# A six-layer cross network on one core: VectorE's order in layer five, the third round of the last layer by pairs of blocks, and the queue of one store

## The chip, the core and the metric

The kernel runs on one core of a Trainium2 chip. The core has five engines with a queue each: TensorE (PE in the profile; PEld are its weight loads), VectorE (DVE), ScalarE (ACT), GpSimd (POOL) and SyncE (SP), which here only issues DMAs. Engines run independently and wait for each other through semaphores. Sixteen DMA engines move data between the chip's memory and the core's own; SP and ScalarE issue to them. The metric is the device time of one execution in microseconds (us), the median of several runs.

## What is computed

`x0` is 4096 rows by 416 columns, `ws` six matrices of 416 x 416, `bs` six vectors of 416, all bfloat16.

```
def reference(x0, ws, bs):
    x = x0
    for l in range(ws.shape[0]):
        x = x0 * (x @ ws[l] + bs[l]) + x
    return x
```

The kernel uses that every x is x0 times something: with c the sum of all (x @ w + b) so far, plus one, x = x0 * c. Each layer adds its product and bias to c (CM, CR in the code) and multiplies by x0 for the next layer's input (XH, XR).

## The kernel before

**Layers one to five, transposed.** In these layers features lie on the partitions and rows of the batch along the free dimension. The 416 features are three blocks m of 128 (XM0, XH, CM) and a remainder of 32 (XR, CR). The 4096 rows are two halves s of 2048, each of two tiles h of 1024. For each (s, m), TensorE fills two PSUM tiles `pt`. ScalarE adds the bias and writes `t`. VectorE adds `t` to CM (the sum) and multiplies CM by XM0 into the next layer's XH.

**Layer five (`feeding_layer`, l = 4)** feeds the last layer, whose blocks have batch rows on the partitions and features along the free dimension. So c must also be turned: for each (s, m), `rows_out` adds the last layer's bias to CM in place on VectorE (L348; for the second half of the batch only half of the columns, since there the last layer's bias comes from matmuls of `bLr` for the other blocks) and issues a DMA transpose into `XLrows` on SP's queue (L231). The remainder goes through `rem_out`, `scrR` and a copy by ScalarE (`xl_rem`). VectorE's order in this layer is written out by hand (L381 to L421) with the helpers `add` (the sum, L340), `mul` (the product, L344), `rows_out`, `rem` and `rem_out`; `pin` keeps instructions in program order. The six tiles (s, m) are called A, Bt, C (first half) and Dt, E, F (second half). The profile's VectorE rows of this layer are L340, L344, L348, L373 and L375.

**Layer six (l = LL)** works in four rounds over `quads`, pairs (s, i): each q stands for four blocks of 128 rows, one for each g. A round takes two values of q, so eight blocks u = 0 to 7. `bank[u]` is the PSUM place of block u; PAIRS, TURNS and ENDS say which half of which of four PSUM tiles that is. In PAIRS two successive blocks are neighbours in one tile; in TURNS (third round) and ENDS (fourth round) most are not. TensorE computes x @ w for each block (`mm_q_open`, `mm_q_full`, `mm_q_rem`).

For each one or two blocks, `close` calls `ew`: ScalarE casts PSUM into `t` (L505), VectorE adds XLrows (the sum, L507), and `close_product` then issues the product of the blocks before (with X0rows into `o`, L495) and its store (L496). So on VectorE the sum of one block comes before the product of the one before it. In rounds one and two blocks are closed two at a time (832 wide), in round three the first two together and then six by one (416 wide), in round four all by one. In the last round the blocks 5 to 7 get c through TensorE (`adds`), so that they need no sum, and block 7 is multiplied straight from PSUM (`direct`).

**Queues.** SP issues, in this order: transpose of A, remainder of the first half, Bt, remainder of the second half, C, Dt, E, F; then 22 stores. ScalarE's queue issues the last store, after its last cast. Buffers: six `t` (tpool), ten `o` (opool), four PSUM tiles of two banks. Completion semaphores of DMAs are eight in rotation: a store waits for the landing of the DMA that was issued eight before it.

Of the kernel before, what the change touches and what calls it, by code (L numbers as in the profile page):

```python
# [10 lines left out]
ALU = mybir.AluOpType  # L11
# [5 lines left out]
def kernel(  # L17
# [7 lines left out]
    nc = tc.nc  # L25
    B, D = x0.shape
# [19 lines left out]
    out_v = out.rearrange("(bt p) d -> p bt d", p=P)  # L46
# [11 lines left out]
    X0rows = big.tile([P, NBT, D], BF16)  # L58
# [11 lines left out]
    def col0(s, g):  # L70
        return SW * s + CW * g
# [8 lines left out]
    def pin(ins):  # L80
        tc.keep_in_program_order(ins)
# [33 lines left out]
    for g in range(1, NG):  # L115
        dst, src = WR[32 * g:32 * g + 32, 0, :], WR[0:R, 0, :]
# [113 lines left out]
    def xl_dmat(s, k):  # L230
        nc.sync.dma_start_transpose(out=XLrows[:, 16 * s:16 * s + 16, 128 * k:128 * k + 128],  # L231
                                    in_=CM[:, k, SW * s:SW * s + SW])
# [73 lines left out]
    def xl_rem(s):  # L306
        dst = XLrows[:, 16 * s:16 * s + 16, NK * P:D].rearrange("p (g i) r -> p i g r", g=NG)
        src = scrR[s][:].rearrange("p i (g r) -> p i g r", g=NG)
        n = 4 if s else 2
        for i in range(0, 4, n):  # L310
            pin(nc.scalar.copy(dst[:, i:i + n], src[:, i:i + n]))
# [13 lines left out]
    def feeding_layer(l, cur, curR, nxt, nxtR):  # L325
        tiles = [(s, m) for s in range(NS) for m in range(NK)]
        pts, ts = {}, {}

        def evict(t):
            for h in range(2):  # L330
                ts[t + (h,)] = tpool.tile([P, 2 * CW], BF16, name="t")
                nc.scalar.activation(ts[t + (h,)][:], pts[t][h][:].rearrange("p a b -> p (a b)"), ACT.Identity,  # L332
                                     bias=bM[:, t[1], l:l + 1], scale=1.0)

        def c_of(t, h):
            c0 = col0(t[0], 2 * h)
            return CM[:, t[1], c0:c0 + 2 * CW]

        def add(t, h):
            pin(nc.vector.tensor_tensor(out=c_of(t, h), in0=ts[t + (h,)][:], in1=c_of(t, h), op=ALU.add))  # L340

        def mul(t, h=0, n=2):
            c0, w = col0(t[0], 2 * h), n * CW
            pin(nc.vector.tensor_tensor(out=nxt[t[0]][:, t[1], 2 * CW * h:2 * CW * h + w], in0=CM[:, t[1], c0:c0 + w],  # L344
                                        in1=XM0[:, t[1], c0:c0 + w], op=ALU.mult))

        def last_bias(c, bias):
            pin(nc.vector.tensor_scalar(out=c, in0=c, scalar1=bias, scalar2=None, op0=ALU.add))  # L348

        def rows_out(t):  # L350
            s, m = t
            c = CM[:, m, SW * s:SW * s + SW]
            if s:
                c = c.rearrange("p (g r) -> p g r", g=NG)[:, :, 0:CW // 2]
            last_bias(c, bM[:, m, LL:L])
            xl_dmat(s, m)

        A, Bt, C, Dt, E, F = tiles
        layer_products(l, 0, tiles, pts, cur, curR, evict)
        evict(Bt)  # L360
        pr2 = psum.tile([P, 2, CW], FP32, tag="ps", name="pr2")
        for s in range(NS):
            mm_rem(l, s, pr2[:, s, :], cur, curR)
        tr = []
        for s in range(NS):
            tr.append(tpool.tile([P, 2 * CW], BF16, name="t"))
            for a in range(0, CW, CW // 2):
                nc.scalar.activation(tr[s][:, a:a + CW // 2], pr2[:, s, a:a + CW // 2], ACT.Identity, bias=bR[:, l:l + 1], scale=1.0)

        def rem(s, op):  # L370
            part = slice(CW * s, CW * s + CW)
            if op == ALU.add:
                pin(nc.vector.tensor_tensor(out=CR[:, part], in0=tr[s][:, 0:CW], in1=CR[:, part], op=op))  # L373
            else:
                pin(nc.vector.tensor_tensor(out=nxtR[:, part], in0=CR[:, part], in1=XR[0][:, part], op=op))  # L375

        def rem_out(s):
            last_bias(CR[:, CW * s:CW * s + (CW // 2 if s else CW)], bR[:, LL:L])
            nc.sync.dma_start_transpose(out=scrR[s][:], in_=CR[:, CW * s:CW * s + CW])

        add(A, 0)  # L381
        mul(A, 0)
        add(A, 1)
        add(Bt, 0)
        mul(A, 1)
        rows_out(A)
        add(Bt, 1)
        rem(0, ALU.add)
        mul(Bt, 0, 4)
        rem(0, ALU.mult)  # L390
        rem(1, ALU.add)
        rem_out(0)
        rows_out(Bt)
        rem(1, ALU.mult)

        layer_products(l, 2, tiles, pts, cur, curR, evict)
        evict(Dt)
        add(C, 0)
        add(C, 1)
        rem_out(1)  # L400
        mul(C, 0, 4)
        add(Dt, 0)
        rows_out(C)
        add(Dt, 1)
        mul(Dt, 0, 4)

        def before_last(t):
            xl_rem(0)
            evict(t)

        layer_products(l, 4, tiles, pts, cur, curR, before_last)
        evict(F)
        add(E, 0)
        rows_out(Dt)
        add(E, 1)
        mul(E, 0, 4)
        add(F, 0)
        rows_out(E)
        add(F, 1)
        mul(F, 0, 4)  # L420
        rows_out(F)  # L421
        xl_rem(1)

    cur, curR = XH[0:2], XR[1]
    for l in range(1, LL):
        nxt, nxtR = [[h for h in XH if h is not cur[0] and h is not cur[1]][0], cur[0]], XR[1 + (l % 2)]
        if l == LL - 1:
            feeding_layer(l, cur, curR, nxt, nxtR)
            cur, curR = nxt, nxtR
            break  # L430
        tiles = [(s, m) for s in range(NS) for m in range(NK)]
        pts = {}

        def finish(t):
            for h in range(2):
                ew_main(l, t[0], t[1], h, pts[t][h], nxt)

        for n in range(0, len(tiles), 2):
            layer_products(l, n, tiles, pts, cur, curR, finish)
            finish(tiles[n + 1])  # L440
            if n == 0:
                rem_pair(l, cur, curR, nxtR)
        cur, curR = nxt, nxtR

    l = LL
# [37 lines left out]
    pending = []  # L483

    def rows(q, g0, n):
        s, i = quads[q]
        b0 = 16 * s + 4 * g0 + i
        return slice(b0, b0 + 4 * (n - 1) + 1, 4)

    def close_product():  # L490
        while pending:
            src, q, g0, n, eng = pending.pop()
            b = rows(q, g0, n)
            o = opool.tile([P, 2, D], BF16, name="o")
            pin(nc.vector.tensor_tensor(out=o[:, 0:n, :], in0=src, in1=X0rows[:, b, :], op=ALU.mult))  # L495
            eng.dma_start(out_v[:, b, :], o[:, 0:n, :])  # L496

    def ew(q, g0, n, src, eng, added, direct):
        if direct:
            close_product()  # L500
            pending.append((src, q, g0, n, eng))
            return
        t = tpool.tile([P, 2 * CW], BF16, name="t")
        tv = t[:, 0:n * D].rearrange("p (a d) -> p a d", a=n)
        nc.scalar.copy(tv, src)  # L505
        if not added:
            pin(nc.vector.tensor_tensor(out=tv, in0=tv, in1=XLrows[:, rows(q, g0, n), :], op=ALU.add))  # L507
        close_product()
        pending.append((tv, q, g0, n, eng))

    PAIRS = [(0, 0), (0, 1), (1, 0), (1, 1), (2, 0), (2, 1), (3, 0), (3, 1)]
    TURNS = [(0, 0), (0, 1), (1, 0), (2, 0), (3, 0), (1, 1), (2, 1), (3, 1)]
    ENDS = [(0, 0), (1, 0), (2, 0), (0, 1), (3, 0), (1, 1), (2, 1), (3, 1)]
    rounds = [(0, PAIRS, 2), (2, PAIRS, 2), (4, TURNS, 2), (6, ENDS, 1)]
    for q, at, done in rounds:
        tiles = [psum.tile([P, 2, CW], FP32, tag="ps", name=f"py{n}") for n in range(4)]
        bank = [tiles[n][:, a, :] for n, a in at]

        final = q + 2 == NQ

        def close(u, n):
            tl, a = at[u]
            ew(q + u // 4, u % 4, n, tiles[tl][:, a:a + n, 0:D], nc.scalar if final and u == 7 else nc.sync,
               final and u >= 5, final and u == 7)

        for u in range(done):
            if q == 0:
                mm_q_open(q, u, bank[u])
            else:
                mm_q_full(q, u, bank[u], False)  # L530
        mm_q_rem(q, bank[0:4], done)
        close(0, done)
        mm_q_rem(q + 1, bank[4:8], 0)
        for u in range(done, 8):
            mm_q_full(q + u // 4, u % 4, bank[u], True, final and u >= 5)
            if at is not PAIRS:
                close(u, 1)
            elif u % 2:
                close(u - 1, 2)
    close_product()  # L540


# [28 lines left out]
```

## Time and profile before

| what | value |
|---|---|
| median of 3 runs | 129.75 us (129.72 to 129.80) |
| the profiled execution | 129.89 us, span 128.1 us |
| granted TensorE clock, mean | 0.997 |
| PE busy | 122.5 us (96%) |
| DVE busy | 102.9 us (80%) |
| ACT busy | 87.7 us (68%) |
| L495, 832 wide, x9 / 416 wide, x13 | 587 ns / 377 ns each |
| L507, 832 wide, x9 / 416 wide, x11 | 587 ns / 375 ns each |
| L505 cast, 832 wide, x9 / 416 wide, x13 | 855 ns / 506 ns each |
| stores on SP's queue | 9 of 208 KB, 13 of 104 KB |

The span is the time from the first to the last instruction of the profiled execution. Busy time counts instructions that run, not waits. PE's busy share says little by itself: matmuls overlap, and their ends are modelled. Instructions on VectorE and ScalarE overlap their neighbours a little, so the time that one adds to a full engine is its start-to-start distance, not its duration. In the timelines, a line gives the start, the length, the engine, the code line, the operation, output and inputs, and how many instructions were merged ("x2"); in square brackets is idle time before it and what ended it.

### The profile page before, as it was taken

How to read it: one execution, taken by the hardware profiler on the slowest of the kernel's cores; microseconds unless marked ns; L12 is line 12 of the kernel's file. 1: busy time of each engine (PE TensorE's matmuls, PEld its weight loads, DVE VectorE, ACT ScalarE, POOL GpSimd, SP SyncE). 2: the span in 40 equal slices, each digit the busy share in tenths (PEclk: the TensorE clock that was granted, in tenths of full speed). 3: DMA queues.
4: the chain of work that ended last, by engine and by line, in shares of the span. 5: the costliest groups of instructions: out<-in, count | busy, mean ns of one | idle time of the engine just before them, and what ended most of it. 6: DMA issues, size and time to landing. Idle time of an engine off the chain costs nothing.

```text
span 128.1 us, 3968 instructions
## 1 busy us (share of the span) xinstructions
PE 122.5 (96%) x1684; PEld 55.3 (43%) x1686; DVE 102.9 (80%) x198; ACT 87.7 (68%) x109; POOL 5.6 (4%) x18
## 2 busy tenths in 40 slices
PE   7999999999999999999999999999999999999960
PEld 3343343444445444444444445444444345445530
DVE  0124579774979898989898989898999999999990
ACT  0038867887858667858667858667859697679740
POOL 4004002500000000000000000000000000000000
PEclk9999999999999999999999999999999999999998
DMA  3999999999950000000000000000089999999764
GB/s 99 232 229 223 178 235 263 304 331 335 339 155 0 5 0 0 8 0 5 0 5 0 5 0 5 0 0 5 0 164 91 176 168 213 157 303 292 248 199 142
DMA packets 42230, 16.38 MB, mean 128 GB/s; under 512 B 31034, under 2 KB 42212, under 8 KB 42212
## 3 DMA queue, kind: packets, MB, share of 16 engines
q1 hardware_dynamic: 37432, 15.40, 53.2%
q10 hardware_dynamic: 4780, 0.72, 3.6%
q8 instruction: 13, 0.21, 0.7%
q14 instruction: 5, 0.04, 0.1%
HBM read 6.15 MB, written 3.41 MB: 75 GB/s over the span
## 4 chain that ended last, share of the span: by engine, by line
PE 86%; DMA 4%; DVE 3%; ACTq 2%; issue 1%; ACT 0%; DVEq 0%
PE pt L208 50%; PE ph L240 11%; PE py L463 10%; PE pt L214 5%; PE pr L224 5%; DMA xrig<-in_x_dram 4%; DVE t L507 2%; PE pr L220 2%; PE ph L247 1%; PE py L476 1%; DVE o L495 1%; PE py L457 1%; ACTq L86 1%; ACTq L108 1%; ACT t L505 0%
## 5 line engine op out<-in xcount | busy, mean ns | idle before, releaser
L208 PE MATMUL pt<-XH,WM 128*32 128x512 bf16 x1152 | 65.2, 379 | 0.0
L187 ACT ACTIVATE t<-pt,bM 128x1024 bf16<-128x1024 f32 x36 | 37.2, 1115 | 13.7 <-PE pt L214 13.7
L208 PEld LDWEIGHTS <-WM 128*32 128x32 bf16 x1152 | 29.7, 97 | 33.8 <-issue 5.1
L188 DVE TENSOR_TENSOR CM<-t,CM 128x1024 bf16<-128x1024 bf16 x36 | 24.7, 687 | 4.3 <-ACT t L187 4.3
L189 DVE TENSOR_TENSOR XH<-CM,XM 128x1024 bf16<-128x1024 bf16 x36 | 24.9, 692 | 2.6
L505 ACT CAST t<-py 128x416 bf16<-128x416 f32 (+1 forms) x22 | 14.2, 649 | 4.2 <-PE py L463 1.8
L463 PE MATMUL py<-WM,XH 128*128 128x416 bf16 x90 | 17.0, 339 | 0.0
L240 PE MATMUL ph<-XM,WM 128*128 128x512 bf16 x70 | 16.3, 379 | 0.3 <-DMA XM<-in_x_dram 0.2
L332 ACT ACTIVATE t<-pt,bM 128x1024 bf16<-128x1024 f32 x12 | 12.4, 1115 | 4.1 <-PE pt L214 4.1
L181 ACT ACTIVATE CM<-ph,bM 128x1024 bf16<-128x1024 f32 x12 | 12.5, 1114 | 3.5 <-PE ph L247 3.5
L183 DVE TENSOR_TENSOR XH<-CM,XM 128x512 bf16<-128x512 bf16 x24 | 8.9, 434 | 4.0 <-ACT CM L181 3.9
L463 PEld LDWEIGHTS <-XH 128*128 128x128 bf16 x90 | 8.5, 98 | 7.5 <-issue 1.2
L240 PEld LDWEIGHTS <-WM 128*128 128x128 bf16 x72 | 6.8, 98 | 8.7 <-issue 1.3
L495 DVE TENSOR_TENSOR o<-t,X0rows 128x416 bf16<-128x416 bf16 (+1 forms) x22 | 9.9, 463 | 0.0
L507 DVE TENSOR_TENSOR t<-t,XLrows 128x416 bf16<-128x416 bf16 (+1 forms) x20 | 9.3, 470 | 0.1
L340 DVE TENSOR_TENSOR CM<-t,CM 128x1024 bf16<-128x1024 bf16 x12 | 8.1, 687 | 0.3 <-ACT t L332 0.3
L344 DVE TENSOR_TENSOR XH<-CM,XM 128x2048 bf16<-128x2048 bf16 (+1 forms) x7 | 7.5, 1070 | 0.4
L214 PE MATMUL pt<-XR,WR 32*128 32x512 bf16 x96 | 7.3, 379 | 0.0
L224 PE MATMUL pr<-XH,WM 128*32 128x512 bf16 x96 | 6.6, 379 | 0.0
L196 ACT ACTIVATE t<-pr,bR 128x256 bf16<-128x256 f32 x12 | 4.7, 475 | 1.6 <-PE pr L224 1.6
L114 ACT ACT_TABLE_LOAD x1 | 1.3, 1283 | 6.1 <-DMA XM<-in_x_dram 6.1
L224 PEld LDWEIGHTS <-WM 128*32 128x32 bf16 x120 | 3.2, 97 | 3.2
(61 smaller groups left out, 59.2 us busy)
## 6 DMA issues: line engine op xcount, KB each, us to landing
X0rows<-in_x_dram SPq DMA_DIRECT2D x8, 312.0 KB, 6.7
out_dram<-o SPq DMA_DIRECT2D x9, 208.0 KB, 3.0
WM<-in_ws_dram SPq DMA_DIRECT2D x5, 312.0 KB
out_dram<-o SPq DMA_DIRECT2D x13, 104.0 KB, 1.9
X0rows<-in_x_dram SPq DMA_DIRECT2D x4, 208.0 KB, 6.3
WR<-in_ws_dram SPq DMA_DIRECT2D x4, 130.0 KB, 5.4
WM<-in_ws_dram ACTq DMA_DIRECT2D x1, 312.0 KB
XM<-in_x_dram SPq DMA_TRANSPOSE x8, 5.7
```

The source lines that it names most:

```text
L181: nc.scalar.activation(c, src, ACT.Identity, bias=bias, scale=1.0)
L187: nc.scalar.activation(t[:], src, ACT.Identity, bias=bias, scale=1.0)
L188: nc.vector.tensor_tensor(out=c, in0=t[:], in1=c, op=ALU.add)
L189: nc.vector.tensor_tensor(out=x, in0=c, in1=XM0[:, m, c0:c0 + 2 * CW], op=ALU.mult)
L208: nc.tensor.matmul(pts[g // 2][32 * q:32 * q + 32, g % 2, :], lhsT=WM[:, l, k, 128 * m + 32 * q:128 * m + 32 * q + 32], rhs=cur[s][:, k, C ...
L214: nc.tensor.matmul(pts[g // 2][:, g % 2, :], lhsT=WR[32 * g:32 * g + 32, l, 128 * m:128 * m + 128], rhs=curR[32 * g:32 * g + 32, CW * s:CW ...
L224: nc.tensor.matmul(pr[32 * g:32 * g + 32, :], lhsT=WM[:, l, k, NK * P:D], rhs=cur[s][:, k, CW * g:CW * g + CW], start=False, stop=(k == NK ...
L240: nc.tensor.matmul(pt[:, gl, :], lhsT=WM[:, 0, k, 128 * m:128 * m + 128], rhs=cur[:, k, c0:c0 + CW], start=(k == 0 and not after_row), sto ...
L332: nc.scalar.activation(ts[t + (h,)][:], pts[t][h][:].rearrange("p a b -> p (a b)"), ACT.Identity, bias=bM[:, t[1], l:l + 1], scale=1.0)
L463: nc.tensor.matmul(py[:, 0:D], lhsT=q_x(q, g, k), rhs=WM[:, l, k, :], start=((not closes) and k == 0), stop=(closes and not adds and k == ...
L505: nc.scalar.copy(tv, src)
L507: pin(nc.vector.tensor_tensor(out=tv, in0=tv, in1=XLrows[:, rows(q, g0, n), :], op=ALU.add))
```

## The change

- In layer five, the second half's sum of a tile now comes before the `rows_out` that stood in front of it (for A with Bt, C with Dt, E with F). `rows_out(F)` leaves the layer: `feeding_layer` returns it, and it is called in round one of the last layer, behind the first `close`, so behind the first sum L507 (L511 in the changed file).
- `ew` takes a list of PSUM sources. For round three (TURNS) two blocks are closed together: two casts of 416 into one `t`, one sum and one product of 832, and two stores of one block each. Rounds one, two and four are as before.
- In the last round the store of block 6 goes to ScalarE's queue, as that of block 7 did.

```diff
         add(A, 1)
         add(Bt, 0)
         mul(A, 1)
+        add(Bt, 1)
         rows_out(A)
-        add(Bt, 1)
         rem(0, ALU.add)
...
         add(Dt, 0)
+        add(Dt, 1)
         rows_out(C)
-        add(Dt, 1)
         mul(Dt, 0, 4)
...
         add(F, 0)
+        add(F, 1)
         rows_out(E)
-        add(F, 1)
         mul(F, 0, 4)
-        rows_out(F)
         xl_rem(1)
+        return lambda: rows_out(F)
...
         while pending:
-            src, q, g0, n, eng = pending.pop()
-            b = rows(q, g0, n)
+            src, q, g0, n, parts, eng = pending.pop()
             o = opool.tile([P, 2, D], BF16, name="o")
-            pin(nc.vector.tensor_tensor(out=o[:, 0:n, :], in0=src, in1=X0rows[:, b, :], op=ALU.mult))
-            eng.dma_start(out_v[:, b, :], o[:, 0:n, :])
-
-    def ew(q, g0, n, src, eng, added, direct):
+            pin(nc.vector.tensor_tensor(out=o[:, 0:n, :], in0=src, in1=X0rows[:, rows(q, g0, n), :], op=ALU.mult))
+            for j in range(0, n, parts):
+                eng.dma_start(out_v[:, rows(q, g0 + j, parts), :], o[:, j:j + parts, :])
+
+    def ew(q, g0, srcs, eng, added, direct):
         if direct:
             close_product()
-            pending.append((src, q, g0, n, eng))
+            pending.append((srcs[0], q, g0, 1, 1, eng))
             return
         t = tpool.tile([P, 2 * CW], BF16, name="t")
+        n = 0
+        for src in srcs:
+            w = src.shape[1]
+            nc.scalar.copy(t[:, n * D:n * D + w * D].rearrange("p (a d) -> p a d", a=w), src)
+            n += w
         tv = t[:, 0:n * D].rearrange("p (a d) -> p a d", a=n)
-        nc.scalar.copy(tv, src)
         if not added:
             pin(nc.vector.tensor_tensor(out=tv, in0=tv, in1=XLrows[:, rows(q, g0, n), :], op=ALU.add))
         close_product()
-        pending.append((tv, q, g0, n, eng))
+        pending.append((tv, q, g0, n, n // len(srcs), eng))
...
-        def close(u, n):
-            tl, a = at[u]
-            ew(q + u // 4, u % 4, n, tiles[tl][:, a:a + n, 0:D], nc.scalar if final and u == 7 else nc.sync,
-               final and u >= 5, final and u == 7)
+        def close(groups):
+            u, direct = groups[0][0], final and groups[0][0] == 7
+            srcs = [tiles[at[g[0]][0]][:, at[g[0]][1]:at[g[0]][1] + len(g), 0:D] for g in groups]
+            ew(q + u // 4, u % 4, srcs, nc.scalar if final and u >= 6 else nc.sync,
+               final and u >= 5, direct)
...
-        close(0, done)
+        close([range(done)])
+        if q == 0:
+            last_rows_out()
...
-            if at is not PAIRS:
-                close(u, 1)
+            if at is ENDS:
+                close([[u]])
             elif u % 2:
-                close(u - 1, 2)
+                close([[u - 1, u]] if at is PAIRS else [[u - 1], [u]])
```

More of the change, by code (lines that the diff above doesn't have):

```diff
@@ L427 @@
         if l == LL - 1:
-            feeding_layer(l, cur, curR, nxt, nxtR)
+            last_rows_out = feeding_layer(l, cur, curR, nxt, nxtR)
             cur, curR = nxt, nxtR
```

## The prediction, made before the changed kernel had run

> **What bounds the kernel now.** I read the page first, then the chain of waits, then the timelines of VectorE, ScalarE and SP's queue over the last 35 us. The page's slices (3.2 us each; PE, DVE and DMA rows) say where to look:
>
> ```profile
> PE   7999999999999999999999999999999999999960
> DVE  0124579774979898989898989898999999999990
> DMA  3999999999950000000000000000089999999764
> ```
>
> TensorE is full until the last two slices. VectorE is full over the last eleven, and the DMA engines are full for ten of these. The chain gives the end:
>
> ```profile
> 114.69 3.80 PE py L463 x21
> ...
> 119.08 0.52 ACT t L505
> ...
> 119.63 0.38 DVE t L507
> ...
> 124.28 0.79 DVE o L495 x2
> ```
>
> Up to about 119 us it runs through TensorE, then through one cast and then only through VectorE's sums (L507) and products (L495). VectorE's timeline shows how close together these stand, and what layer five costs just before (start, duration):
>
> ```profile
> 99.47 0.75 DVE L348 TENSOR_SCALAR CM<-CM,bM 128x2048 bf16<-128x2048 bf16 x1
> 100.14 0.68 DVE L340 TENSOR_TENSOR CM<-t,CM 128x1024 bf16<-128x1024 bf16 x1
> 100.92 1.23 DVE L344 TENSOR_TENSOR XH<-CM,XM 128x2048 bf16<-128x2048 bf16 x1
> ...
> 106.78 1.23 DVE L344 TENSOR_TENSOR XH<-CM,XM 128x2048 bf16<-128x2048 bf16 x1
> 108.05 0.49 DVE L348 TENSOR_SCALAR CM<-CM,bM 128x1024 bf16<-128x1024 bf16 x1
> 108.59 1.09 DVE L507 TENSOR_TENSOR t<-t,XLrows 128x832 bf16<-128x832 bf16 x2
> 109.60 0.59 DVE L495 TENSOR_TENSOR o<-t,X0rows 128x832 bf16<-128x832 bf16 x1
> ...
> 117.13 0.37 DVE L507 TENSOR_TENSOR t<-t,XLrows 128x416 bf16<-128x416 bf16 x1
> 117.42 0.59 DVE L495 TENSOR_TENSOR o<-t,X0rows 128x832 bf16<-128x832 bf16 x1
> 117.92 0.37 DVE L507 TENSOR_TENSOR t<-t,XLrows 128x416 bf16<-128x416 bf16 x1
> ...
> 124.48 0.59 DVE L495 TENSOR_TENSOR o<-py,X0rows 128x416 bf16<-128x416 f32 x1
> ```
>
> Independent neighbours overlap by 0.08 us: a 0.59 us pair costs 0.50, a 0.37 us single 0.285, a 0.69 us sum 0.60. A neighbour that works on what the one before it has just touched does not overlap: L344 at 100.92 starts 0.78 after its own sum, not 0.60. VectorE lags behind ScalarE, whose casts set how far it can catch up:
>
> ```profile
> 114.54 4.05 ACT L505 CAST t<-py 128x832 bf16<-128x832 f32 x7 [0.49 <-PE py L476]
> 119.08 0.51 ACT L505 CAST t<-py 128x416 bf16<-128x416 f32 x1 [0.48 <-PE py L480]
> 119.98 2.09 ACT L505 CAST t<-py 128x416 bf16<-128x416 f32 x4 [0.39 <-PE py L463]
> 122.27 0.51 ACT L505 CAST t<-py 128x416 bf16<-128x416 f32 x1 [0.20 <-PE py L469]
> 122.99 0.51 ACT L505 CAST t<-py 128x416 bf16<-128x416 f32 x1 [0.21 <-PE py L469]
> ```
>
> The last cast ends at 123.50 and TensorE's last product about 123.67 (L469 starts at 123.49 and takes 0.18), but the VectorE product that needs the latter starts only at 124.48. So the tail is VectorE's by 0.8 us, and that 0.8 is all that less VectorE work can bring. SP's queue is one line of transposes and stores:
>
> ```profile
> 101.06 11.13 SPq L231 DMA_TRANSPOSE XLrows<-CM  x4
> 112.29 13.23 SPq L496 DMA_DIRECT2D out_dram<-o  x22
> ```
>
> It issues its last store, the last but one of the kernel, from 125.12 to 125.52, beside ScalarE's only one (125.10 to 125.50).
>
> **The change, part by part.** Times are of the profiled execution: 129.89 us in all, its span 128.1 (128.07 to the last record), 1.8 around it; the median shown, 129.75, is 0.14 below.
>
> *Layer five.* The same instructions stand in another order. The gaps that vanish are those between dependent neighbours: L348 of A behind L344 of A (91.66, where 91.55 would do: 0.11); L344 of D behind its sum (0.18); the same for F (106.78 for 106.60: 0.18); L348 of F behind L344 of F (108.05 for 107.92: 0.13); the first L507 behind that (0.54 after its start, where such an L348 takes 0.40, from 102.67 to 103.06: 0.14). Together 0.74. Against it, the second sum of C waits for its cast: it starts at 96.93 now and the cast ends at 96.86, so 0.07 is lost. Net 0.67: the second sum of round one comes at 108.42 instead of 109.10. The bounds are 0 (nothing is added, and the transposes below are covered) and 0.74; I take 0.67, since each gap is read off the line itself. The inputs of layer six (L344) are ready earlier too, which brings nothing: no group of TensorE's matmuls there idles.
>
> What is moved past it: the transposes. A's L348 ends 0.5 us later; SP then issues nothing from 94.23 to 95.49, waiting for the remainder's bias, so that is covered, and without that idle time 0.5 would pass on to all later transposes. C's bias (a sum of 0.60 later, 0.04 gained by then) would end at 100.78, just before SP's queue is free at about 100.9. E's (0.60 later, 0.22 gained) ends at 106.46 instead of 106.08, and SP waits for it: 0.38 late, and F's transpose and the first store with it (112.67 for 112.29). F's bias now stands behind the first sum, which needs the transposes of A, B and C; C's must land by 107.5, when the sum would start (L344 of F at 106.38, plus 1.14). The transposes issued at 92.44 and 97.31 landed after 5.8 and 4.4 us, so one issued at 100.95 lands by 106.8: covered by 0.7, and each us more would be a us of VectorE. F's bias ends at 108.4, before SP has issued E's transpose (109.2): no cost. The first sum that needs F's transpose comes at 115.45; issued at 109.3 with 5.8 us it lands at 115.1.
>
> *Third round in pairs.* Of the round's seven sums and seven products one each is a pair already. Between 117.13 and 120.77 stand eleven singles and one pair: 11 x 0.285 + 0.50 = 3.64. Instead six pairs, 6 x 0.50 = 3.01, and the last product costs 0.50 for 0.285: 0.63 - 0.22 = 0.41 saved. ScalarE's casts stay as they are, and so do the stores, one block each. A pair's sum waits for two casts. The seven casts from 114.54 end at 115.40, 115.86, 116.39, 116.92, 117.44, 117.97 and 118.60 (pitch 0.53); with the lead of 0.67 the pairs' sums would come at 116.46, 117.48 and 118.63, the last two on the heels of their casts. Bounds 0.41 and, with no lead to spend, the same.
>
> *Last round.* With both gains (1.08) VectorE would run ahead of the casts: sums at 119.63, 120.52, 121.09, 121.66 and 122.23, products of units 3 to 5 at 122.52, 122.80 and 123.09. The product of unit 6 waits for its cast (123.50) until 123.53; unit 7's follows at 123.82, 0.15 behind TensorE, and ends at 124.41 instead of 125.07. So 0.66 of 1.08 reaches the end; 0.41 alone would give 124.67.
>
> *Last but one store on ScalarE's queue.* It is issued at about 123.95 for 0.40, behind all casts, so that only the last store (ready at 124.44) stands behind it: no delay. SP's queue ends one issue (0.49 pitch) earlier, at about 124.5. No row shows two stores in a row on ScalarE's queue. The nearest: stores issued on SP at 123.74 and 124.17 landed after 1.7 us, and the last two, issued at the same moment, kept the DMA engines busy until 127.0 (their share is 0.00 from there on), which makes about 2.0. Bounds 0 and 0.3; I take 0.15, the middle, since the stores no longer start together but still share the DMA engines. The Trainium skill says in "DMA: Bandwidth & Descriptors", section "Issuing engines are not separate DMA queues", that several issuing engines save only the sequencer's time to initiate; by it this part brings 0 and the sum is 0.15 less.
>
> *Sum:* 0.66 + 0.15 = 0.81 off 129.89, 129.08 in a profile; off the median 129.75, **128.95 us**.
>
> **The rivals.**
> *The order in layer five brings nothing.* For it: a gap might only turn up elsewhere. Against: independent neighbours overlap in every row shown. Then 0.41 stays, 124.67 for VectorE's end: 129.75 - 0.41 = **129.34**. The Trainium skill has such a rule in "VectorE: DVE Perf Modes", section "The DRAIN you can't avoid": the next operation waits for the empty pipe whether or not a semaphore lies between. The rows at 100.14 and 100.92 disagree with that, 0.60 against 0.78.
>
> *The DMA engines bound the end.* Their share is 1.06 from 112 to 118 us. The store of 113.98 landed after 4.3 us, that of 118.03 after 3.5, of 119.75 after 2.7, of 122.65 after 1.9: a backlog that drains only as single stores come more slowly than they are served. The stores now start 0.38 later and come earlier at the end. The ninth store landed at 118.03 + 3.5 = 121.5 and the third after it at 119.75 + 2.7 = 122.45, 0.32 each. From 121.5 + 0.38, fourteen singles at 0.32 end at 126.4, level with the forecast's 127.1 - 0.8 = 126.3. With each at 0.36 (one eighth more) it is 126.9, and 0.2 is left of the gain: **129.55**, no change.
>
> *Slower: the backlog holds the queues.* Every store waits for the landing of the one eight before, and the last but one store now stands ahead of the last on ScalarE's queue. The one eight before it is the fifth after the ninth: 121.88 + 5 x 0.32 = 123.5, 0.45 before it is needed. Once that landing slips by more than 0.45 both wait, us for us, and past 1.25 us of slip the end lies behind today's. For it: the landing time jumped from 2.5 to 4.3 us between the stores of 113.43 and 113.98; one more such jump of 1.8 there costs 1.35: 128.95 + 1.35 = **130.3**. Against: nothing in the change adds bytes, and that jump came where the engines were full.
>
> **How the numbers follow.** Forecast 0.62, no gain from the order 0.17, DMA-bound 0.13, slower 0.05; 0.03 is left for a larger gain (the full 0.8 of the tail and the 0.3). The forecast's own bounds, 0.66 + 0 to 0.66 + 0.3 and up to 0.1 of the slack behind TensorE, give 128.7 to 129.1. The range 128.65 to 129.6 takes in the first two rivals and leaves about 0.1 out. A measurement of this kernel tells 0.2%, 0.26 us, from no change, so faster means below 129.49: forecast, first rival, the larger gain and a third of the second, 0.86; same 0.08; slower 0.06.
>
> **What would show it.** L344 of D and F 0.60 to 0.67 after their predecessor; the second sum near 108.4; six 832-wide instructions between the ninth product's neighbours; no VectorE gap over 0.1 in the third round; the last product at 123.8; two issues on ScalarE's queue near 123.95 and 124.45; the first store near 112.7. It is wrong if VectorE idles before the first sum (C's transpose), if the last product still starts past 124.2, or if it starts at 123.8 and the span still ends past 127.7.

## The result, and the profile after

| | before | after |
|---|---|---|
| median of 22 runs each | 129.79 us (129.64 to 130.32) | 129.50 us (129.30 to 129.77) |
| ratio, 95% interval | | 0.9977 (0.9971 to 0.9983) |
| profiled execution | 129.89, span 128.1 | 129.49, span 127.7 |
| VectorE's last product | 124.48 to 125.07 | 123.83 to 124.42 |
| SP's last store issued / ScalarE's last | 125.12 / 125.10 | 124.34 / 124.45 |
| last landing | 127.21 | 126.69 |

The changed kernel is faster by 0.22 to 0.38 us, where 0.8 was forecast. VectorE did what was forecast; less than half of the gain forecast for the end arrived there. The page's slices of the changed kernel (3.2 us each, tenths busy):

```profile
PE   7899999999999999999999999999999999999970
DVE  0123579874979898989898989898999999999990
DMA  3999999999950000000000000000098899899864
```

VectorE is as full over the last eleven slices as before. The DMA engines' row has changed: five nines near the end where there were seven, and an 8 for a 7 from 118 to 121 us. VectorE's timeline (start, duration) shows the edits one by one:

```profile
98.84 1.28 DVE L340 TENSOR_TENSOR CM<-t,CM 128x1024 bf16<-128x1024 bf16 x2
100.05 0.74 DVE L348 TENSOR_SCALAR CM<-CM,bM 128x2048 bf16<-128x2048 bf16 x1
100.71 1.22 DVE L344 TENSOR_TENSOR XH<-CM,XM 128x2048 bf16<-128x2048 bf16 x1
...
107.51 0.58 DVE L511 TENSOR_TENSOR t<-t,XLrows 128x832 bf16<-128x832 bf16 x1
108.01 0.48 DVE L348 TENSOR_SCALAR CM<-CM,bM 128x1024 bf16<-128x1024 bf16 x1
108.41 0.58 DVE L511 TENSOR_TENSOR t<-t,XLrows 128x832 bf16<-128x832 bf16 x1
...
117.49 0.59 DVE L511 TENSOR_TENSOR t<-t,XLrows 128x832 bf16<-128x832 bf16 x1
118.54 0.59 DVE L511 TENSOR_TENSOR t<-t,XLrows 128x832 bf16<-128x832 bf16 x1
...
123.83 0.58 DVE L494 TENSOR_TENSOR o<-py,X0rows 128x416 bf16<-128x416 f32 x1
```

L344 of D (100.71) now starts 0.66 after its predecessor instead of 0.78. The second sum comes at 108.41 (108.42 was forecast), the third round's sums are pairs right behind their casts, and the last product starts at 123.83, 0.65 earlier than before. ScalarE's timeline has its last cast and the two stores:

```profile
123.00 0.51 ACT L507 CAST t<-py 128x416 bf16<-128x416 f32 x1 [0.17 <-PE py L469]
123.95 0.86 ACTq L496 DMA_DIRECT2D out_dram<-o  x2
```

The chain of waits no longer ends in a run of VectorE's sums and products. It goes through TensorE, the last cast and a single product, and from there into the closing waits:

```profile
119.32 2.39 PE py L463 x13
...
123.00 0.52 ACT t L507
...
123.54 0.07 DVE o L494
```

So VectorE is out of the way, yet the end moved by 0.40 (127.67 for 128.07 in the records). The windows of one us each (window, length, busy PE, PEld, DVE, ACT, POOL, granted clock, DMA share, GB/s) show what the DMA engines do then, first before:

```profile
122.00:123.00 1.00, 1.00 (x12) 0.69 (x11) 1.00 (x5) 0.58 (x3) 0.00 (x0) 1.00 0.48 147
...
125.00:126.00 1.00, 0.00 (x0) 0.00 (x0) 0.07 (x1) 0.00 (x0) 0.00 (x0) 1.00 0.67 216
126.00:127.00 1.00, 0.00 (x0) 0.00 (x0) 0.00 (x0) 0.00 (x0) 0.00 (x0) 1.00 0.70 221
```

and after:

```profile
122.00:123.00 1.00, 1.00 (x12) 0.67 (x11) 1.00 (x5) 0.63 (x2) 0.00 (x0) 1.00 0.52 171
...
125.00:126.00 1.00, 0.00 (x0) 0.00 (x0) 0.00 (x0) 0.00 (x0) 0.00 (x0) 1.00 1.00 306
126.00:127.00 1.00, 0.00 (x0) 0.00 (x0) 0.00 (x0) 0.00 (x0) 0.00 (x0) 1.00 0.17 57
```

Before, the stores trickle at 0.7 until the end. After, they bunch: a whole us at share 1.00, after four stores left within 0.61 us, two on SP's queue (123.84, 124.34) and two on ScalarE's (123.95, 124.45). Both have a us at half share before that (122 to 123). SP's queue shows where the hole comes from (the same timeline, cut at three windows; SPq is an issue on SP's queue):

```profile
111.76 0.94 SPq L496 DMA_DIRECT2D out_dram<-o  x1
120.59 0.88 SPq L496 DMA_DIRECT2D out_dram<-o  x2
121.01 1.29 SPq L496 DMA_DIRECT2D out_dram<-o  x2
```

Two successive issues take 0.88 together at 120.59, but 1.29 at 121.01: the queue stands still for 0.44 between 121.53 and 121.97, although the product that this store carries was done at 121.19. In the trace of before the same stop lies between its 14th and 15th store (121.22 to 121.67). The line of 22 merged stores that the prediction quoted hides it.

### The profile page after: what moved, and what is told of

Read it like the earlier page. It is cut to its first block, busy times and chain, and to the rows that moved or that the text cites. A ratio compares the mean times of both kernels' runs of the same rounds, so it can differ in the third digit from the quotient of the medians.

```text
span 127.7 us, 3953 instructions
## 1 busy us (share of the span) xinstructions
PE 122.4 (96%) x1684; PEld 55.3 (43%) x1686; DVE 102.6 (80%) x192; ACT 87.8 (69%) x109; POOL 5.0 (4%) x18
## 4 chain that ended last, share of the span: by engine, by line
PE 90%; DMA 4%; ACTq 2%; DVEq 1%; ACT 0%; issue 0%; DVE 0%
PE pt L208 50%; PE py L463 12%; PE ph L240 11%; PE pt L214 5%; PE pr L224 5%; DMA xrig<-in_x_dram 4%; PE pr L220 2%; PE py L476 2%; PE ph L247 1%; PE py L457 1%; ACTq L86 1%; DVEq L573 1%; ACTq L108 1%; ACT t L507 0%; ACTq L74 0%
## 5 line engine op out<-in xcount | busy, mean ns | idle before, releaser
L507 ACT CAST t<-py 128x416 bf16<-128x416 f32 (+1 forms) x22 | 14.2, 649 | 4.2 <-PE py L463 2.0
L494 DVE TENSOR_TENSOR o<-t,X0rows 128x832 bf16<-128x832 bf16 (+1 forms) x19 | 9.4, 503 | 0.1
L511 DVE TENSOR_TENSOR t<-t,XLrows 128x832 bf16<-128x832 bf16 (+1 forms) x17 | 8.9, 522 | 0.0
L344 DVE TENSOR_TENSOR XH<-CM,XM 128x2048 bf16<-128x2048 bf16 (+1 forms) x7 | 7.5, 1066 | 0.2
```

The lines of the kernel that those rows point to most:

```text
L507: nc.scalar.copy(t[:, n * D:n * D + w * D].rearrange("p (a d) -> p a d", a=w), src)
```

## The experiments

Each ratio is to runs of the kernel before beside it on the same chip; in brackets is its 95% interval. The theories that the expectations name: V, VectorE's gain reaches the end whole; L, the landings of the last stores, a third of a us each, set the end; Q, formed on the way, SP's queue sets it, at 0.48 us for each store issued back to back plus one stop of 0.44.

### Each part alone

**Order of layer five alone** (the kernel before with these moves):

```diff
+        add(Bt, 1)
         rows_out(A)
-        add(Bt, 1)
...
+        add(Dt, 1)
         rows_out(C)
-        add(Dt, 1)
...
+        add(F, 1)
         rows_out(E)
-        add(F, 1)
...
-        rows_out(F)
+        return lambda: rows_out(F)
...
         close(0, done)
+        if q == 0:
+            last_rows_out()
```

> The kernel before with the new order of layer five alone (F's bias behind the first sum as well); third round by single blocks, last but one store on SP. Both theories: VectorE's last product starts near 123.8 and ends near 124.4 instead of 125.07, since the lead of 0.67 alone carries it to the last cast. Theory L (the landings of the last stores set the end, at about a third of a us each, and pass on only a part of VectorE's gain): 0.2 to 0.4 us faster than before. Theory V (VectorE's gain reaches the end whole, and in the changed kernel the store on ScalarE's queue takes some of it back): 0.55 to 0.7 faster.

129.27 us, ratio 0.9958 (0.9945 to 0.9970): more than the whole change brought. By the medians (0.60 faster) this is in theory V's range and above L's. VectorE's timeline and ScalarE's store:

```profile
123.78 0.58 DVE L495 TENSOR_TENSOR o<-py,X0rows 128x416 bf16<-128x416 f32 x1
...
124.39 0.41 ACTq L496 DMA_DIRECT2D out_dram<-o  x1
```

The last product stands where the whole change has it (123.83). The last store of SP leaves at 124.55 and the last landing is at 126.50.

**Third round in pairs alone** (with `close` and `ew` as in the change):

```diff
-            if at is not PAIRS:
-                close(u, 1)
+            if at is ENDS:
+                close([[u]])
             elif u % 2:
-                close(u - 1, 2)
+                close([[u - 1, u]] if at is PAIRS else [[u - 1], [u]])
```

> The kernel before with the third round in pairs alone. Both: VectorE ends near 124.67, 0.40 earlier than before. Theory L: 0.1 to 0.25 us faster. Theory V: 0.35 to 0.45 faster.

129.96 us, ratio 1.0012 (1.0004 to 1.0020): slightly slower, where both theories expected a gain, and although VectorE ends 0.55 earlier. VectorE's last product and SP's single stores:

```profile
123.93 0.58 DVE L494 TENSOR_TENSOR o<-py,X0rows 128x416 bf16<-128x416 f32 x1
...
119.11 6.70 SPq L496 DMA_DIRECT2D out_dram<-o  x13
```

The kernel before issues the same thirteen from 118.60 on, in 6.92:

```profile
118.60 6.92 SPq L496 DMA_DIRECT2D out_dram<-o  x13
```

A pair's product gives out its first store only when both blocks are done, so the queue starts 0.51 later. After that it waits for VectorE only once, for 0.12: 13 x 0.48 + 0.44 = 6.68, measured as 6.70. SP's last issue starts at 125.42 instead of 125.12. (In these two executions the last landings are level, 127.20 and 127.21; that the pairs cost time alone rests on the medians.) In the kernel before, VectorE ended at 125.07 and SP's last store left at 125.12: two chains that ended together, and this part moves the second the wrong way. That is theory Q.

**The store of block 6 on ScalarE's queue alone** (this part of one line):

```diff
-nc.scalar if final and u == 7 else nc.sync,
+nc.scalar if final and u >= 6 else nc.sync,
```

> The kernel before with the last but one store on ScalarE's queue alone. Both: VectorE's end stays at 125.07. Theory L: the last three stores still land one after the other; between 0.1 slower and 0.1 faster. Theory V: the last store, now second on ScalarE's queue, lands 0.2 to 0.3 later after its issue: 0.1 to 0.3 slower.

130.27 us, ratio 1.0031 (1.0019 to 1.0042), slower than either theory expected. ScalarE's timeline:

```profile
124.69 1.14 ACTq L496 DMA_DIRECT2D out_dram<-o  x2
```

Two issues take 1.14 here and 0.86 in the changed kernel: ScalarE stands still for 0.33 right before the last store, which leaves at 125.47 instead of 125.10.

### One part taken out of the change

**The change with block 6's store back on SP** (`u >= 6` becomes `u >= 7`):

> The changed kernel with the last but one store back on SP's queue. Both: VectorE ends at 124.41 as in the changed kernel. Theory L: SP's queue, which issues one store in 0.48 us, ends 0.5 later than in the changed kernel, so 0.0 to 0.2 us slower than it (0.1 to 0.3 faster than before). Theory V: 0.2 to 0.3 faster than the changed kernel (0.5 to 0.6 faster than before).

129.57 us, ratio 0.9974 (0.9962 to 0.9987), against 0.9977 for the change: no gain of the store's queue is seen here, as theory L expected and not V. With these intervals a gain of 0.1 us could not be told from none. Against the order alone (0.9958) the pairs cost about 0.2 us, but the intervals overlap.

**The change without pairs** (`if at is ENDS:` becomes `if at is not PAIRS:`):

> The changed kernel with round three by single blocks (order of layer five and the store on ScalarE's queue, no pairs). Theory Q: SP's twelve singles from 118.21 end near 124.5, 0.5 before those of the kernel with the order alone; the last store on ScalarE's queue is held by 0.3 us, as in the kernel with the store alone, where ScalarE stopped just before it: 129.2 to 129.5. Theory L: as the kernel with the order alone, 129.2 to 129.35.

129.63 us, ratio 0.9986 (0.9975 to 0.9997), above what either expected. SP's last store leaves at 124.15, yet ScalarE's timeline shows its stop again before the last store:

```profile
123.95 1.12 ACTq L496 DMA_DIRECT2D out_dram<-o  x2
```

That store leaves at 124.72 and lands 2.28 later, at 127.00. With two stores on ScalarE and round three by single blocks the stop falls there; in the changed kernel, where ScalarE's trace records three instructions fewer, it falls into the closing steps instead.

### Issues on SP's queue, fewer and more

**The change with one store of 208 KB for each pair of round three:**

```diff
-        pending.append((tv, q, g0, n, n // len(srcs), eng))
+        pending.append((tv, q, g0, n, n, eng))
```

> The changed kernel with one store of 208 KB for each pair of round three instead of two of 104 KB: three issues fewer on SP, the same bytes. Theory Q (SP's queue sets the end: from the first single store on it issues one in 0.47 to 0.48 us back to back, with one stop of 0.44 us at a fixed place in its instructions): SP is no longer back to back in round three, its last store is issued by 124.1 instead of 124.34, and the last landing comes 0.2 to 0.5 us earlier: 129.0 to 129.3. Theory L (the DMA engines' own rate sets the landings at the end): same bytes at the same rate, 129.4 to 129.6.

129.28 us, ratio 0.9960 (0.9948 to 0.9972). Same work on VectorE, same bytes, three issues less: SP's last store leaves at 124.16 and the last landing is at 126.50. By the median Q's size is met; the profiled execution is the slowest of the five, 129.49.

**The same with block 6's store on SP** (`u >= 7`):

> One store for each pair of round three, and the last but one store on SP. Theory Q: SP's last store is issued near 124.5 (one issue after the 124.1 of e5), level with ScalarE's 124.45, without ScalarE's stop in its closing steps: 129.0 to 129.3, as e5. Theory L: 129.4 to 129.6.

129.46 us, ratio 0.9973 (0.9962 to 0.9983), a miss for Q and in L's range, though the interval overlaps that of the one above. The last landing is at 126.50 in both, and in both more time than before's 0.86 lies behind it, 1.05 here and 1.17 above. SP closes with five waits in a fixed order, each for two semaphores. In before the last to land is in the fourth; here it is in the first and above in the second, and the waits behind it, 0.065 each, still come. Above, ScalarE's stop adds 0.18 in the closing steps. What makes the medians differ by 0.18 is open.

**Order alone, singles on VectorE, round three's six single stores as three of two blocks** (two products go into the halves of one `o`, one store behind the second):

> The kernel with the order of layer five alone (e1), sums and products of round three by single blocks, but its six single stores issued as three of two blocks. VectorE's last product is held by the last cast as in e1. Theory Q: SP has three issues fewer; its last store is issued near 124.5 as in e8 and e1, so 129.2 to 129.5: as e8, which has the same stores with VectorE's work in pairs, within 0.15. If pairs on VectorE were themselves worth something at the end, e8 would be faster than this by 0.2 or more.

129.46 us, ratio 0.9967 (0.9956 to 0.9979), as expected and equal to the one above within the intervals. With equal stores, pairs or singles on VectorE make no difference that can be told.

**One issue more:** the change with block 6's store on SP and a transfer of 4 bytes, unused, behind one store of the last round:

```diff
+            if (q, g0) == (6, 2):
+                nc.sync.dma_start(spare[0:1, :], o[0:1, 0, 0:2])
```

> The changed kernel with the last but one store back on SP (e4) and one more DMA issue on SP in the last round, of 4 bytes, between two stores. Theory Q: everything behind it on SP is issued 0.45 later, and the end with it: 0.35 to 0.5 us slower than e4, 129.9 to 130.1. Theory L: 4 bytes cost nothing, 129.5 to 129.65.

129.88 us, ratio 1.0010 (0.9999 to 1.0021): 0.0036 or 0.47 us above the same kernel without it (129.57; by medians 0.31), far from L's range and just below Q's. SP's queue:

```profile
122.37 0.51 SPq L497 DMA_DIRECT2D out_dram<-o  x1
122.93 0.72 SPq L499 DMA_DIRECT2D spare<-o  x1
123.75 1.79 SPq L497 DMA_DIRECT2D out_dram<-o  x4
```

This issue holds the queue for 0.82 us (122.93 to 123.75), longer than a store's 0.48, and the end comes 0.3 to 0.5 us later, though 4 bytes ask nothing of VectorE and almost nothing of the DMA engines. The extra transfer also shifts the stores by one semaphore: the last to land is now in the third closing wait instead of the fourth, which explains 0.05 of it. This is the clearest support for Q.

**The first four stores of the last round as two as well,** with block 6's store on SP, then on ScalarE:

```diff
+            if q == NQ - 2:
...
+                j = g0 % 2
+                pin(nc.vector.tensor_tensor(out=o[:, j:j + 1, :], in0=src, in1=X0rows[:, rows(q, g0, n), :], op=ALU.mult))
+                if j:
+                    eng.dma_start(out_v[:, rows(q, g0 - 1, 2), :], o[:])
+                continue
```

> e8 (one store for each pair of round three, last but one store on SP) with the first four stores of the last round issued as two of two blocks as well: SP has two issues fewer in the last 2 us, its last store is issued near 123.95 to 124.1, straight after its product. Theory Q: the last landing is then that of ScalarE's store, 0.2 to 0.3 earlier than in e8: 129.1 to 129.3. If the DMA engines' rate holds the landings (theory L): as e8, 129.4 to 129.55.

> As e10, with the last but one store on ScalarE's queue. SP is done by 123.6. Theory Q: no gain over e10, since SP no longer is what is late, and ScalarE's stop of 0.35 at a fixed place in its instructions falls into the closing steps as in the changed kernel: 129.2 to 129.45, 0.0 to 0.2 slower than e10. Theory L: as e5, 129.3.

129.76 us (0.9991, 0.9981 to 1.0001) and 129.94 us (1.0003, 0.9990 to 1.0017): both missed, on the slow side. The stop now falls right before block 4's store (123.27 to 123.71 in the first), and the data of the bigger stores comes out later, so that much is still on its way at the end (argued from the traces, not tried); both land last at 126.9. Fewer issues alone are not the cure, and Q alone does not give these times.

### The stop, moved

In before, in the changed kernel and in all experiments the stop precedes the same place on SP, the 80th instruction that the trace records there, whichever store that is. Loading X0rows in more pieces, early and far from the end, puts more instructions ahead of it:

```diff
-    for q in range(12):
-        b0, b1 = NBT * q // 12, NBT * (q + 1) // 12
+    for q in range(28):
+        b0, b1 = NBT * q // 28, NBT * (q + 1) // 28
```

**20 pieces,** on the order alone, on the change, and on the change with block 6's store on SP:

> The kernel with the order of layer five alone (e1), and X0rows loaded in 20 pieces instead of 12, early in the kernel where SP has time. SP then has 16 instructions more ahead of its stores; the stop of 0.44 us, if it belongs to the 80th of SP's recorded instructions, moves eight stores forward, to a store for whose product SP waits anyway. Theory Q: SP's last store is issued at about 124.1 instead of 124.55, and the end comes 0.2 to 0.35 earlier than in e1: 128.9 to 129.1. If the stop belongs to the store and not to the place, or SP is not what is late: as e1, 129.2 to 129.35.

> The changed kernel with X0rows loaded in 20 pieces. Theory Q: SP's last store is issued near 123.9 instead of 124.34, ahead of both of ScalarE's; the last landing is ScalarE's, at 124.45 + 1.8 to 2.0 instead of 2.24: 0.2 to 0.4 earlier than in the changed kernel, 129.1 to 129.3 (ScalarE's own stop stays in the closing steps). If SP's stop does not count: 129.4 to 129.55.

> Order and pairs, last but one store on SP (e4), with X0rows loaded in 20 pieces. Theory Q: SP's last store is issued near 124.4 instead of 124.86, level with ScalarE's: 0.25 to 0.4 earlier than e4, 129.1 to 129.35. If the stop does not count: as e4, 129.5 to 129.6.

129.36 (0.9962, 0.9948 to 0.9977), 129.49 (0.9973, 0.9962 to 0.9984) and 129.44 us (0.9970, 0.9958 to 0.9983): each equal to its kernel with 12 pieces, and each above what Q expected. The stop moved by four stores only, to the 11th, still among stores issued close together: the eight more pieces are eight more recorded instructions on SP, not the sixteen expected. These runs also show that more pieces by themselves bring nothing.

**28 pieces,** on the same three:

> As e12 (order of layer five alone), with X0rows in 28 pieces. In e12 the 80th instruction was the 11th store, still among the stores that SP issues back to back; eight instructions more put it on the 7th, where SP waits for a product. Theory Q: SP's last store near 124.1 to 124.2 instead of 124.55, and the end 0.2 to 0.35 earlier than e1: 128.9 to 129.1. If SP's queue is not what holds the last landing: 129.2 to 129.4.

> The changed kernel with X0rows in 28 pieces. Theory Q: SP's last store near 123.9 instead of 124.34, last landing ScalarE's store: 129.1 to 129.3. Otherwise 129.4 to 129.55.

> Order and pairs, last but one store on SP (e4), with X0rows in 28 pieces. Theory Q: SP's last store near 124.4 instead of 124.86: 129.1 to 129.35. Otherwise 129.45 to 129.6.

The stop is now before the 7th store. It still delays that one (in the change with 28 pieces the product is done at 115.66 and the stop ends at 116.04), but early enough: SP waits 0.36 for a product again before the store of 118.75. The order alone: 129.15 us, ratio 0.9952 (0.9940 to 0.9965), 0.9958 without, between Q's range and the other. The change: 129.23 us, 0.9951 (0.9938 to 0.9964), 0.9977 (0.9971 to 0.9983) without. The change with block 6's store on SP: 129.20 us, 0.9962 (0.9949 to 0.9976), 0.9974 without. These two are in Q's ranges. Only for the change do the intervals part: 0.0026, some 0.33 us (0.15 to 0.5). SP's queue of that kernel, first the moved stop and then its twelve last stores:

```profile
115.02 1.47 SPq L496 DMA_DIRECT2D out_dram<-o  x2
118.75 5.80 SPq L496 DMA_DIRECT2D out_dram<-o  x12
```

The changed kernel's own twelve take 0.32 more:

```profile
118.61 6.12 SPq L496 DMA_DIRECT2D out_dram<-o  x12
```

Its windows have lost the hole, and less is left over for the last us:

```profile
122.00:123.00 1.00, 1.00 (x13) 0.69 (x12) 1.00 (x5) 0.77 (x2) 0.00 (x0) 1.00 0.70 229
...
125.00:126.00 1.00, 0.00 (x0) 0.00 (x0) 0.00 (x0) 0.00 (x0) 0.00 (x0) 1.00 0.95 307
126.00:127.00 1.00, 0.00 (x0) 0.00 (x0) 0.00 (x0) 0.00 (x0) 0.00 (x0) 0.71 0.05 16
```

From 122 to 123 it moves 229 GB/s where the changed kernel moves 171: 0.06 MB, half a store, that need not be moved at the end. The last landing comes at 126.55 instead of 126.69, although VectorE's last product ends 0.14 later in this execution (124.56): ScalarE's last store lands 1.96 after its issue (124.59) instead of 2.24.

No run tried what the stop is, but the traces give a hint. They also hold the packets of the DMA queues that the page calls "instruction". In every kernel the next load of 8 KB on queue q14 starts 0.6 to 1.5 us after the end of SP's stop, and it moves with the stop:

| kernel | SP's stop | next load on q14 |
|---|---|---|
| before | 121.22 to 121.67 | 122.57 |
| changed | 121.53 to 121.97 | 122.60 |
| changed, 20 pieces | 119.03 to 119.47 | 120.12 |
| changed, 28 pieces | 115.59 to 116.04 | 117.49 |

Behind ScalarE's stop there is such a load too (124.40 to 124.72 and 125.76 in the change without pairs). So the stops seem to belong to the loading of an engine's own instructions; that is a reading of the times, not shown.

## Why the prediction was half right

**Layer five: right.** The lead of 0.67 was read off the gaps, and 0.69 came (108.41 for 109.10). The order alone is worth 0.0042 or 0.55 us (0.39 to 0.71 by the interval), so the rival by which it brings nothing is out. It had the Trainium skill's "VectorE: DVE Perf Modes", section "The DRAIN you can't avoid", beside it. That section also says "A next op that is not held starts earlier", which the prediction left out; the rows of 0.66 after the move and 0.78 before it, and this run, agree with that. The covers held as well: C's transpose was in time for the first sum, and E's, issued at 106.49 (106.46 forecast), delayed no sum. The first store left at 111.76, not at 112.7, because the issue of F's transpose took 1.99 instead of 3.27.

**Third round in pairs: saving right, worth wrong.** VectorE was freed as worked out. But with the lead of layer five already there, the last casts hold VectorE (the prediction's own 0.66 of 1.08), so that the pairs could bring nothing at the end. Their price was not seen: the stores of a pair come out together and later, and SP's queue has little slack to take that up. Alone they cost 0.16 us (0.05 to 0.26).

**VectorE's end: right.** 124.41 was forecast and 124.42 came, with ScalarE's issues at 123.95 and 124.45 to the hundredth.

**The step that failed** is the one behind VectorE's end: that its 0.66 "reaches the end", with 0.15 more from the store. The last issue did come 0.67 earlier (124.45 for 125.12). But from there to its landing the last store took 2.24 instead of 2.09, so 0.15 was lost where 0.15 was to be gained, and from landing to end it took 0.98 instead of 0.86, 0.12 that the sum put at nothing. In the profiles 0.67 - 0.15 - 0.12 = 0.40 arrived of 0.81. Behind the landing term stands "SP's queue ends one issue (0.49 pitch) earlier, at about 124.5". It took SP's queue for a line that follows VectorE, and did not count the stop of 0.44 that the trace of before already has. In the changed kernel twelve stores at about 0.48 and that stop made SP end at 124.73, so that its last two stores met ScalarE's two. With the stop moved the landing took 1.96. The prediction also read the DMA row as full for ten slices; it shows an 8, seven nines and then 7, 6 and 4.

**The 0.15 for the store's queue: not seen** (0.9977 against 0.9974, with intervals that would hide it), and 0.40 us lost by itself. That fits the Trainium skill's "DMA: Bandwidth & Descriptors", section "Issuing engines are not separate DMA queues", which the prediction set beside it. The SP time saved was real (its last issue 0.5 earlier, 124.34 for 124.86), but the transfers met at share 1.00.

**How much is settled.** The stop accounts for about 0.33 us (0.15 to 0.5): that is shown by moving it, in one kernel, with 20 pieces as the control; in the other two the gains of 0.08 and 0.16 are not resolved. With 28 pieces the change stands at 0.64 us below before; the last 0.17 to the forecast is only argued from traces: three stores served a third of a us apart, landings of 2.0 to 2.3 us, and ScalarE's stop of 0.32 to 0.36, which now falls in the closing steps. SP's longest wait for another queue there is 0.56 in all five kernels where ScalarE's stop falls there, and 0.38 in all others, also in the two where it falls before ScalarE's last store. That stop was not moved by itself. The DMA-bound rival gave 129.55, next to the 129.50 measured, but part of that is luck: it put the last landing at 126.9, which came at 126.69, and left out the closing. Its mechanism is part of the cause: 4 bytes more on the queue cost 0.3 to 0.5 us, so the engines alone don't set the end, but with the stop out of the way they still run at share 0.95 from 125 to 126, so their rate is a bound there too.

The rival on the slower side, a jump in the landings that holds the queues, did not occur. The versions that beat both kernels are the change with 28 pieces, 129.23 us, and the order of layer five with 28 pieces, 129.15 us. The second does without pairs and without the store on ScalarE.

## What to carry to other kernels

When one engine ends last by a few tenths of a us, look for the next chain that ends as late, and count a queue's issues one by one, not by a merged line: here a line of 22 merged stores hid a stop of 0.44 us and a queue that ended within 0.1 us of VectorE. Work done in pairs saves time on its engine but hands on its results later and together, which is a loss if a queue behind it is full. A part that is worth 0.55 us alone can be worth half with two others beside it, so the parts should be run alone.

## What the runs showed of the hardware that was not expected

- SP's queue stands still for 0.43 to 0.45 us before the 80th instruction that its trace records, in all 19 kernels, whatever that instruction is. ScalarE does so for 0.32 to 0.36 us before its 192nd recorded one in the seven kernels with two stores on its queue; in five more the 192nd comes where ScalarE waits for another queue anyhow, and the other seven record fewer. The cause is not shown; a load of 8 KB on an instruction queue follows each stop of SP by 0.6 to 1.5 us.
- In the last round SP issues stores of 104 KB 0.4 to 0.5 us apart when it waits for no product (122.41, 122.87, 123.36, 123.84, 124.34 in the changed kernel), while the DMA engines finish one in about 0.35 us (106 KB at 306 GB/s, an estimate). So while one queue issues them, the queue, not the engines, paces small stores (share 0.70); when they bunch, the engines do.
- A store of 104 KB lands 1.7 to 1.8 us after its issue while SP alone issues one behind another, and 1.9 to 2.3 us when the last stores of both queues leave close together.
- SP's closing waits run in a fixed order, 0.065 us each. Which one the last landing ends, and ScalarE's stop, make the time from landing to end anything from 0.80 to 1.23 us (0.86 in before).
